# A transformer block on one core: dilated attention without a row maximum, transposes by DMA, and instruction orders fixed beforehand

**The chip, the cores and the metric.** The kernel runs on one core of one Trainium2 chip. The metric is the device time in microseconds (us), the median of several executions. Engines are written as the profile writes them: PE is TensorE (PEld its weight loads), DVE VectorE, ACT ScalarE, POOL GpSimd, SP the engine that issues DMAs. SBUF and PSUM are the on-chip memories in which the code keeps its tiles; here matmuls read from SBUF tiles and write to PSUM tiles. "Span" is the time from the first to the last record of one profiled execution. PEclk is the share of full clock speed that the throttle granted PE.

## The reference

One block: adaptive layer norm, dilated local attention, output projection with a gated residual, a second adaptive norm, a SiLU MLP and a second gated residual. S = 2048 positions, D = 448, 16 heads of 28, MLP width 1792, everything in bf16.

```python
# cut to what matters; x is A_x, mod the six vectors of silu(c) @ w_mod
h = layernorm(x) * (1 + ca) + sa
q, k, v = split(h @ wqkv)                        # 16 heads of 28
idx = pos[:, None] - 2 * arange(8)[None, :]      # 8 keys: i, i-2, ..., i-14
logits = where(idx >= 0, einsum(q, k[idx]) * 28**-0.5, -1e9)
o = einsum(softmax(logits), v[idx]) @ wo
x = x + ga * o
h = layernorm(x) * (1 + cb) + sb
out = x + gb * (silu(h @ w1) @ w2)
```

An even position looks only at even positions and an odd one only at odd positions. Both kernels use that: each works on two sequences of 1024.

## The kernel before

It splits the even and the odd sequence into blocks of 24 queries that look at 32 keys. A copy spreads four heads over a block-diagonal stationary operand, so a score or value matmul has only 32 columns. The mask is added by a matmul with the identity, the softmax subtracts its row maximum, and DVE transposes values and probabilities.

```python
# attention of one group of four heads, T blocks of 24 queries
nc.tensor.matmul(L[:, 0:T, :], lhsT=ident[:], rhs=mask_bf[...], start=True, stop=False)
for j in range(T):
    nc.tensor.matmul(L[:, j, :], lhsT=S4[:, g, j, :], rhs=kg[:, g, BQ*j:BQ*j+BW], ...)
nc.vector.tensor_reduce(out=mx[:, 0:T], in_=L[:, 0:T, :], axis=AX.X, op=ALU.max)
nc.vector.tensor_tensor(out=xm[...], in0=L[...], in1=mx[...].to_broadcast(...), op=ALU.subtract)
nc.scalar.activation(out=pe[...], in_=xm[...], func=ACTF.Exp, scale=SCALE)
# ... later
nc.vector.tensor_reduce(out=rs[:, 0:T], in_=pe[...], axis=AX.X, op=ALU.add)
nc.vector.reciprocal(out=rs[:, 0:T], in_=rs[:, 0:T])
nc.vector.tensor_tensor(out=pn[...], in0=pe[...], in1=rs[...].to_broadcast(...), op=ALU.mult)
nc.vector.transpose(out=pT[:, 0:T, :], in_=pn[:, 0:T, :])
for j in range(T):
    nc.tensor.matmul(O[:, j, :], lhsT=V4[:, g, j, :], rhs=pT[:, j, :], start=True, stop=True)
# ... cut
```

The set-up scales the weights instead of the activations, before anything uses them, and the first projection comes after all of it:

```python
def late_setup_compute():          # norms of the odd sequence, biases, gates
    ...
    for kt in range(NKT):          # 448 x 1792 weights scaled on ACT
        la(nc.scalar.activation(out=w1_sb[:, kt, :], in_=w1_sb[:, kt, :],
                                func=ACTF.Identity, scale=onep[:, 1, kt:kt+1]))
    ...                            # w2 and wo times their gates on DVE
late_setup_compute()
...
qkv_next = project(0)
for k in range(NGRP + 1):
    ...   # attention of group k, then the MLP of group k-1 as a filler
```

Residuals are added by a matmul with the identity, and the MLP's up projection runs its contraction of 448 as four matmuls of 128 rows, the last of them 64 rows of data and 64 of zeros. Apart from a few chains of dependencies, a scheduler decides the order of each engine.

## Time and profile before

| | before |
|---|---|
| device time, median of four runs | 263.18 us (261.44 to 264.94) |
| span and PEclk of the profiled run | 263.8 us, 0.955 |
| PE / DVE / ACT / POOL busy | 208.8 / 157.2 / 167.4 / 28.7 us |
| first QKV matmul starts | 51.5 us |
| first exponential starts | 65.0 us |
| first MLP matmul starts | 93.2 us |
| last matmul ends | 259.5 us |

The lines themselves stand in the prediction below, taken from the page's 40 slices, from a table of stretches (windows), from the chain of waits and from the groups of instructions. The busy shares alone say little: no engine is over 80%. The landmarks in the lower half cut the span into three: 93.2 us up to the first MLP matmul, 166.3 us from there to the last matmul, and a tail of 4.3 us.

### The profile page before, as it was taken

How to read it: one execution, taken by the hardware profiler on the slowest of the kernel's cores; microseconds unless marked ns; L12 is line 12 of the kernel's file. 1: busy time of each engine (PE TensorE's matmuls, PEld its weight loads, DVE VectorE, ACT ScalarE, POOL GpSimd, SP SyncE). 2: the span in 40 equal slices, each digit the busy share in tenths (PEclk: the TensorE clock that was granted, in tenths of full speed). 3: DMA queues.
4: the chain of work that ended last, by engine and by line, in shares of the span. 5: the costliest groups of instructions: out<-in, count | busy, mean ns of one | idle time of the engine just before them, and what ended most of it. 6: DMA issues, size and time to landing. Idle time of an engine off the chain costs nothing.

```text
span 263.8 us, 4748 instructions
## 1 busy us (share of the span) xinstructions
PE 208.8 (79%) x1902; PEld 131.3 (50%) x1902; DVE 157.2 (60%) x361; ACT 167.4 (63%) x296; POOL 28.7 (11%) x53
## 2 busy tenths in 40 slices
PE   0337425989799289988999969999899565999993
PEld 0336223556466167655655646556675343455651
DVE  5383585579998999589704899028996843000000
ACT  2480376698847856499933999429993548553820
POOL 3860111000000100110001100011001101001001
PEclk9999999999979869999999999999999959599999
DMA  6999400000000100004001030010200030201001
GB/s 227 353 322 312 164 0 0 4 0 2 0 0 2 38 6 2 35 0 62 0 14 42 2 60 2 0 51 6 40 2 17 20 60 15 49 0 46 7 20 35
DMA packets 15840, 13.30 MB, mean 50 GB/s; under 512 B 9225, under 2 KB 13962, under 8 KB 15818
## 3 DMA queue, kind: packets, MB, share of 16 engines
q1 hardware_dynamic: 15050, 11.16, 15.3%
q0 software_dynamic: 768, 1.84, 2.0%
q8 instruction: 15, 0.25, 0.4%
q14 instruction: 7, 0.06, 0.1%
HBM read 9.06 MB, written 1.84 MB: 41 GB/s over the span
## 4 chain that ended last, share of the span: by engine, by line
PE 36%; DVE 27%; issue 19%; ACT 9%; POOL 4%; DMA 3%; POOLq 0%; SPq 0%; ACTq 0%; DVEq 0%
PE ps_h L445 12%; PE ps_y L454 10%; DVE mx L391 4%; PE ps_p L368 3%; DVE xm L393 3%; DVE statsb L180 3%; PE O L422 2%; DVE rs L413 2%; ACT qkv L370 2%; DVE pn L416 2%; PE pst L208 2%; ACT w_sb L333 2%; ACT xn L202 2%; DVE S L380 2%; DMA h2T<-xn 2%
## 5 line engine op out<-in xcount | busy, mean ns | idle before, releaser
L445 PE MATMUL ps_h<-h2T,w_sb 128*128 128x384 bf16 (+1 forms) x336 | 56.1, 325 | 11.4 <-DMA h2T<-xn 6.4
L368 PE MATMUL ps_p<-h1T,w_pad 128*128 128x344 bf16 (+1 forms) x288 | 48.9, 318 | 1.4 <-ACT qkv L370 1.3
L447 ACT ACTIVATE hid<-ps_h,b 128x384 bf16<-128x384 f32 (+1 forms) x84 | 44.0, 547 | 8.9 <-PE ps_h L445 5.9
L445 PEld LDWEIGHTS <-w_sb 128*128 128x128 bf16 x336 | 33.4, 102 | 30.7 <-issue 16.3
L454 PE MATMUL ps_y<-w_sb,hid 128*128 128x448 bf16 x224 | 45.0, 353 | 0.0
L370 ACT ACTIVATE qkv<-ps_p,bq 128x344 bf16<-128x344 f32 (+1 forms) x72 | 35.6, 562 | 4.6 <-PE ps_p L368 4.1
L368 PEld LDWEIGHTS <-w_pad 128*128 128x128 bf16 x288 | 28.3, 100 | 18.2 <-issue 4.2
L454 PEld LDWEIGHTS <-hid 128*128 128x128 bf16 x224 | 21.9, 98 | 19.9
L391 DVE TENSOR_REDUCE mx<-L 128x14 f32<-128x448 f32 (+1 forms) x24 | 14.1, 622 | 28.0 <-PE L L389 27.9
L458 ACT CAST ot<-ps_y 128x448 bf16<-128x448 f32 x16 | 8.5, 532 | 35.0 <-PE ps_y L456 35.0
L202 ACT ACTIVATE xn<-x_all,nmra,rstda 128x448 bf16<-128x448 bf16 x16 | 10.9, 748 | 19.1 <-DVE nmra L190 14.6
L459 POOL DMA_DIRECT2D out_dram<-ot x16 | 9.1, 566 | 124.2 <-ACT ot L458 124.2
L422 PE MATMUL O<-pT,V 128*128 128x32 bf16 x344 | 12.6, 180 | 8.4 <-DVE pT L419 8.4
L434 PE MATMUL ps_o<-wo_pad,oT 128*128 128x448 bf16 x64 | 17.6, 387 | 0.6 <-ACT oT L424 0.6
L422 PEld LDWEIGHTS <-V 128*128 128x128 bf16 x344 | 12.1, 99 | 12.0 <-issue 10.2
L208 PE MATMUL pst<-ident,xn 128*128 128x128 bf16 x64 | 9.3, 308 | 9.7 <-ACT xn L202 8.4
L380 DVE COPY S<-qkv 32x1792 bf16<-32x1792 bf16 (+1 forms) x24 | 14.9, 622 | 1.6 <-ACT qkv L370 1.3
L407 DVE COPY V<-vs 32x1792 bf16<-32x1792 bf16 (+1 forms) x24 | 15.1, 628 | 0.6
L413 DVE TENSOR_REDUCE rs<-pe 128x14 f32<-128x448 f32 (+1 forms) x24 | 14.0, 602 | 1.2 <-ACT pe L396 1.1
L419 DVE STREAM_TRANSPOSE pT<-pn 128x448 bf16<-128x448 bf16 (+1 forms) x24 | 14.6, 634 | 0.1
L416 DVE TENSOR_TENSOR pn<-pe,rs 128x448 bf16<-128x448 f32 (+1 forms) x24 | 14.3, 624 | 0.1
L405 DVE STREAM_TRANSPOSE vs<-qkv 128x448 bf16<-128x448 bf16 (+1 forms) x24 | 14.2, 631 | 0.2
(88 smaller groups left out, 247.0 us busy)
## 6 DMA issues: line engine op xcount, KB each, us to landing
x_all<-in_A_x_dram SPq DMA_DIRECT2D x4, 448.0 KB, 9.5
out_dram<-ot POOLq DMA_DIRECT2D x16, 112.0 KB, 2.0
w_sb<-in_B_w_dram SPq DMA_DIRECT2D x1, 1568.0 KB
wmod_sb<-in_w_mod_dram SPq DMA_DIRECT2D x1, 1344.0 KB
w_sb<-in_B_w_dram SPq DMA_DIRECT2D x1, 1344.0 KB, 11.8
wqkv_st<-in_A_wqkv_dram SPq DMA_DIRECT2D x1, 1008.0 KB
wmod_sb<-in_w_mod_dram SPq DMA_DIRECT2D x1, 672.0 KB, 6.0
wo_pad<-in_A_wo_dram SPq DMA_DIRECT2D x4, 98.0 KB
```

What stands on the lines that cost most here:

```text
L202: wa(nc.scalar.activation(out=xn[:, 0:D], in_=x_all[:, U, :], func=ACTF.Identity, scale=rstd[:, j:j + 1], bias=nmr[:, j:j + 1]))
L368: nc.tensor.matmul(ps[:, 0:wd], lhsT=w_pad[:, kt, typ, g, :], rhs=h1T[:, kt, e0:e0 + wd], start=(kt == 0), stop=(kt == NKT - 1))
L370: nc.scalar.activation(out=tiles[typ][:, g, 0:wd], in_=ps[:, 0:wd], func=ACTF.Identity, bias=bq[:, typ * 4 + g:typ * 4 + g + 1])
L380: nc.vector.tensor_copy(out=_ap4(S4[:, 0, 0, :], 32 * hq, 32 * hq, ((TMAX * 128, NG), (128, T), (1, BW))), in_=_ap4(qg[:, 0, :], 32 * hq, ...
L391: nc.vector.tensor_reduce(out=mx[:, 0:T], in_=L[:, 0:T, :], axis=AX.X, op=ALU.max)
L413: nc.vector.tensor_reduce(out=rs[:, 0:T], in_=pe[:, 0:T, :], axis=AX.X, op=ALU.add)
L416: nc.vector.tensor_tensor(out=pn[:, 0:T, :], in0=pe[:, 0:T, :], in1=rs[:, 0:T].unsqueeze(2).to_broadcast([128, T, BW]), op=ALU.mult)
L422: nc.tensor.matmul(O[:, j, :], lhsT=V4[:, g, j, :], rhs=pT[:, j, :], start=True, stop=True)
L434: nc.tensor.matmul(ps[:, 0:D], lhsT=oT[:, g, n0:n0 + 128], rhs=wo_pad[:, g, :], start=(g == 0), stop=False)
L445: nc.tensor.matmul(ps[:, 0:n], lhsT=w1_sb[:, kt, f * 128:(f + 1) * 128], rhs=h2T[:, kt, c0:c0 + n], start=(kt == 0), stop=(kt == NKT - 1))
L447: ins = nc.scalar.activation(out=hid[:, f, 0:n], in_=ps[:, 0:n], func=ACTF.Silu, bias=b1[:, f:f + 1])
L454: nc.tensor.matmul(ps[:, 0:D], lhsT=hid[:, f, j * 128:(j + 1) * 128], rhs=w2_sb[:, f, :], start=(f == 0), stop=False)
```

## The change

Its intent is to take instructions off PE and DVE, and to leave no engine waiting by chance. The new file shares hardly a line with the old one; these are the pieces that matter, marked as added against what they replace.

```diff
-x_view = A_x...rearrange("(a p two) d -> two a p d", two=2, p=128)
+x_view = A_x...rearrange("(c i p t) d -> c p i (t d)", c=NC, i=2, t=2)  # both parities in one piece
 # scores: one matmul for one head and 112 queries, four heads on four row strips of PE
-    nc.tensor.matmul(L[:, j, :], lhsT=S4[:, g, j, :], rhs=kg[:, g, BQ*j:BQ*j+BW], ...)
-    nc.vector.tensor_reduce(out=mx[...], in_=L[...], axis=AX.X, op=ALU.max)
-    nc.vector.tensor_tensor(out=xm[...], in0=L[...], in1=mx[...], op=ALU.subtract)
-    nc.scalar.activation(out=pe[...], in_=xm[...], func=ACTF.Exp, scale=SCALE)
+    r = 32 * (2 * t + j)
+    T.matmul(held[t][:, j, g*nq:(g+1)*nq], lhsT=qk[r:r+DH, 1, g, par, keys], rhs=qk[r:r+DH, 0, g, par, queries])
+    S.activation(out=out_, in_=ps[...], func=ACTF.Exp, scale=SCALE)         # no row maximum
+    V.tensor_tensor(out=p, in0=p, in1=maskb[...], op=ALU.mult)              # mask of ones and zeros
 # values: a column of ones beside V gives the softmax sum
-    nc.vector.tensor_reduce(out=rs[...], in_=pe[...], axis=AX.X, op=ALU.add)
-    nc.vector.transpose(out=pT[...], in_=pn[...])
+    T.matmul(ps[:, h, 0:DH+1], lhsT=p[:, at:at+128], rhs=v[:, h, 0:DH+1], start=True, stop=True)
+    V.reciprocal(out=r, in_=ps[0:nq, :, DH])
+    V.tensor_tensor(out=box["o"][...], in0=ps[0:nq, :, 0:DH], in1=r..., op=ALU.mult)
+    nc.sync.dma_start_transpose(out=oT[:, :, par, ...], in_=box["o"][0:nq, :])
 # residual: an add on DVE that also gives the sum for the next norm
-    nc.tensor.matmul(ps[:, 0:D], lhsT=ident[:], rhs=x_all[:, U, :], start=False, stop=True)
+    V.scalar_tensor_tensor(out=x_all[:, u+par, :], in0=box["ps"][:, par, 0:D], scalar=1.0,
+                           in1=x_all[:, u+par, :], op0=ALU.mult, op1=ALU.add, accum_out=sums[...])
 # the fourth slice of the contraction (64 rows): two of them, on two halves of PE
+    T.matmul(ps[:, j, :], lhsT=w13[half(j), 128*i:128*i+128], rhs=h[half(j), :, 3, :], ...)
 # ... cut: norms, projections, gates, 11 + 12 throw-away matmuls that warm PE up
+ORDER = "0 4 53 26 27 28 35 1 2 3 40 ..."    # from a search on a model of the engines
+P.emit("" if safe else ORDER)                # "": the order of a list scheduler instead
 # without a maximum a sum could overflow: all sums are checked, and a second program stands behind
+    V.tensor_scalar(out=ok[:], in0=rcf, scalar1=LO, scalar2=None, op0=ALU.is_ge)
 # ... cut
+with tc.If(bad > 0):
+    layer(again, tc, io, True)               # softmax with maximum
```

## The prediction

> **What bounds the kernel now.** I read the 40-slice view first, because a change of this size moves stages and not one wait.
>
> ```profile
> PE   0337425989799289988999969999899565999993
> DVE  5383585579998999589704899028996843000000
> ACT  2480376698847856499933999429993548553820
> PEclk9999999999979869999999999999999959599999
> ```
>
> PE is sparse in the first eight slices, nearly full in the middle and full again in the last six, while DVE is empty at the end: three stages. I cut the windows view at their borders, 57.4 us (first DVE piece of attention) and 221.5 us.
>
> ```profile
> core 0: us, PE busy (x) PEld busy (x) DVE busy (x) ACT busy (x) POOL busy (x), PEclk, DMA share, GB/s
> 0.00:57.40 57.40, 27.54 (x273) 19.80 (x274) 33.00 (x102) 30.92 (x39) 14.48 (x31) 1.00 0.50 159
> 57.40:221.50 164.10, 145.72 (x1448) 92.71 (x1446) 124.04 (x259) 116.03 (x222) 10.88 (x16) 0.95 0.08 19
> 221.50:263.80 42.30, 35.51 (x185) 18.75 (x183) 0.16 (x1) 20.48 (x36) 3.31 (x7) 0.92 0.10 27
> ```
>
> So 57 us are set-up, in which PE is busy half the time and mostly waiting on small work; 164 us are attention and MLP together; 42 us are a last MLP on PE alone. The chain of waits says what holds each.
>
> ```profile
> 11.18 0.71 PE ps_c L238 x13
> ...
> 33.08 3.57 ACT V L306 x4
> ...
> 50.38 5.13 ACT w_sb L333 x3
> ...
> 133.39 2.65 PE ps_y L454 x14
> 136.23 2.65 PE ps_y L454 x14
> ...
> 142.31 1.23 DVE mx L391 x2
> 143.56 0.72 DVE xm L393 x2
> ...
> 151.23 1.14 DVE pn L416 x2
> 152.37 0.60 DVE pT L419
> ```
>
> (start, us, engine, tile, line, count.) In the head the chain runs through scaling weights and zeroing buffers on ACT; the first QKV matmul stands at 51.5 us. In the middle it alternates: MLP matmuls on PE, then some 10 us of softmax on DVE with PE on filler. 14 matmuls of 448 columns start in 2.65 us, 189 ns each; the same group's mean is 353 ns, so about 164 ns of a matmul is tail that the next one covers. I use these spacings below, not the group means.
>
> ```profile
> 108.03 0.86 PE L389 MATMUL L<-qkv,S 128*128 128x32 bf16 x28
> 159.12 8.13 PE ps_h L445 x50
> ```
>
> The first gives (0.86 - 0.18) / 27 = 25 ns for a weight load with a 32-column matmul; the second 163 ns for 384 columns. From 163 to 189 is 0.417 ns a column, so 512 columns are 216 ns, 128 are 56 ns.
>
> **What the Trainium skill says.** "TensorE: Matmul & The Clock Gate", Back-to-back issue gap, has N/2.4 + 2.5 ns: 189 ns at 448, which the trace agrees with. "TensorEngine Tiling (Array Packing)", Key Properties, says that row tiles run independently and that changing the tiling mode drains TensorE; the kernel before has no such tiles, so no run shows it yet, and I rest on it. "ScalarE: Activation LUTs", What ACT_TABLE_LOAD costs, gives 186 ns + 0.833 ns an element, 93 ns more for each pointer operand, and an overlap of 93 ns. The xn activation (448 elements, two pointers) would be 745 ns and takes 748; a plain 448 cast takes 532, a little less than its 559. "VectorE: DVE Perf Modes", Side-by-side, allows tensor_tensor two 16-bit elements a cycle: w2 times its gate, 6272 elements, takes 3.43 us, 0.55 ns each, which agrees.
>
> **The change part by part.** PE first. Before, at these spacings: QKV 192 x 146 + 96 x 156 ns = 43.0; MLP up 48.7; MLP down 42.4; output projection and its residuals 96 x 189 = 18.2; mask matmuls 4.6; score and value matmuls 688 x 25 = 17.2; the rest (transposes, gates, one-column matmuls) about 15. Sum 189 us of a 264 us span; some 75 us are waits and cold clock.
>
> After, from the compiled instruction list. The fourth slice of a 448-long contraction (64 rows) is now run as two matmuls on two halves of the array at once, so 8 cost 7. QK 96 full + 16 pairs = 112 x 216 = 24.2 (keys of one parity only, no 32-for-24 windows). V 63 x 189 = 11.9. Output projection 56 x 189 = 10.6, residual gone into a DVE add. MLP up 196 x 216 = 42.3. MLP down 224 x 189 = 42.4. Scores: 288 matmuls of 28 rows, four at a time, 72 x 50 = 3.6. Values 288 x 25 = 7.2, and the extra column of ones gives the softmax sum. Transposes 64 x 56 = 3.6; gates 1.5; modulation columns 64 x 50 = 3.2. Sum 150.5, 38 less. I count about 101 changes of array mode; at half the 164 ns tail each, an estimate, 8 more: 158.
>
> DVE before was 157 us, of it 8 operations of 0.60 to 0.63 us for each of 24 groups (mx, xm, rs, pn, pT and the copies and transposes for S, V): 115. After, each of 18 blocks has a mask multiply (1792 x 0.55 + fixed = 1.09 by the wo gate row), a reciprocal 0.22 and a normalising multiply 0.62: 18 x 1.93 + 0.3 = 35. Statistics (only of the first norm) 16 x 0.77 = 12, h1 modulation 18 x 0.43 = 8, x1 and output adds 32 x 0.62 = 20, and xn, h2, gates and evacuations about 28. Sum 103. ACT: 32 exponentials of 896 (0.84) and 4 of 1024 (0.95) 30.7, 28 Silus of 1024 26.5, 13 QK evacuations 12.3, 5 V 4.2, 15 xn 9.9, 16 squares 9, seven table loads 9, other 8: 110, from 167. Neither is the bound overall.
>
> By stage. The list fixes each engine's order, so I summed it up to the first MLP matmul. PE has 44.5 us there, of which 3 (32 modulation matmuls, 16 transposes) lie before the first QK matmul; ACT 45; DVE 55. The first QK matmul needs x (first half lands near 3.5 us, as the 448 KB load did at 4.2), 0.84 MB of w_mod and 1.2 MB of wqkv: 2.5 MB. The page's first two slices moved 227 and 353 GB/s, so these are in at 9.5 us, plus about 2 for landing and padding: 12 us against 51.5. This is the largest single gain, some 40 us. From there PE needs 41.5 + 38 mode changes x 0.08 = 44.5, to 57; DVE, starting at 3.5, reaches 58 if it never waits. Three engines so near one another will not all be full, and DVE must wait on GpSimd (its pow takes 0.9 us) and w_mod in the head: I put the first MLP matmul at 64. Then PE has 106 + 63 x 0.08 = 111 us, in which ACT (65) and DVE (48) have room and the MLP's matmuls can fill attention's waits. 64 + 111 = 175; 3 of waits and cold clock; 3 for the last add, store and landing. **181 us**.
>
> Off the path: 26 DMA transposes replace 16. The old ones landed 2.4 us after issue; they replace PE or DVE transposes and lie behind filler. In the last blocks the path score, exponent, mask, values, transpose, projection, norm, transpose, MLP takes some 17 us, and the third MLP chunk (21 us of PE) lies beside it. The sum check and its flag are at the end of the queues and overlap the last 9.9 us of matmuls; the second, safe program is jumped over.
>
> **The rivals.** (1) DVE or ACT takes the bound in the first stage: DVE has 55 us there against PE's 44.5, and the exponents wait for projections. For it: the sums. Against: the order was searched with these durations. Each us that DVE waits moves the end, so 190 to 196. (2) A fixed order is brittle: with five queues in a set order, one late DMA transpose (2.4 us) stops everything behind it, and gaps on PE like those before 217 us bring the low clock that followed them before, where 384-column matmuls start every 0.32 us. That gives 195 to 205. (3) Mode changes cost the whole 164 ns tail: 101 x 0.164 = 17 instead of 8, so 190. If they are hidden, 173. (4) The schedule is as good as the PE sum: 12 + 155 + 3 = 170. (5) The check fails and the safe program runs: well over 300 us; the logits here are of order one and the bounds 1e30 apart, so I give it under 1%.
>
> **Range and chances.** The floor is (4), 170; the likeliest losses are (1) and (3), each about 9, seldom both in full. Eight in ten: 172 to 196. Even (2) stays 20% below 263, so faster is nearly sure.
>
> **What would show it.** First QK matmul near 12 us and first MLP matmul near 64; PE dense from there on with 448-column spacing at 189 ns; the paired 64-row matmuls costing one; DVE near 103 and ACT near 110 us busy; the last DVE add within 3 us of the end. The prediction is wrong if the pairs don't overlap (16 x 0.216 + 9 x 0.189 + 8 x 0.189 + 28 x 0.216 = 13 us more), if the first MLP matmul comes after 75, or if PE after that is under 85% busy.

## The result, and the profile after

The changed kernel took 191.13 us, the median of four runs (190.95 to 191.44), against 263.18 us in the same rounds. The ratio is 0.725, with a 95% interval of 0.721 to 0.729. Ratios here and below are the mean time of one kernel's fast runs over that of the other's of the same rounds, so they are not quite the ratio of the quoted medians. All four runs were fast ones, with PEclk from 0.992 to 0.998.

These are the 40 slices of the changed kernel, one digit for each 4.7 us, in tenths of busy time (PEclk in tenths of full speed).

```profile
PE   7759998889879999999997999979999999999980
DVE  7579989999976630079874401697664022101220
ACT  3145799956976496895736667996189652264000
PEclk9999999999999999999999999999999999999996
```

PE is dense from the fourth slice to the end, and its clock stays at 0.9 or more before the last slice. What was a sparse set-up of eight longer slices is gone: DVE is nearly full through slices 4 to 11, and after that only in two single slices. The same in a table of stretches, cut at the first projection matmul, the first MLP matmul and the last add (busy us of each engine, instructions in brackets, then PEclk, share of the DMA engines and GB/s):

```profile
core 0: us, PE busy (x) PEld busy (x) DVE busy (x) ACT busy (x) POOL busy (x), PEclk, DMA share, GB/s
0.00:13.60 13.60, 9.31 (x72) 4.47 (x74) 8.97 (x31) 4.21 (x7) 5.18 (x26) 1.00 0.86 271
13.60:30.00 16.40, 15.42 (x116) 6.57 (x116) 15.12 (x38) 13.11 (x16) 8.19 (x26) 1.00 1.04 330
30.00:50.00 20.00, 18.22 (x286) 10.38 (x284) 18.92 (x38) 16.34 (x22) 1.40 (x4) 1.00 0.19 45
50.00:65.80 15.80, 14.44 (x128) 6.35 (x124) 11.20 (x23) 10.61 (x19) 2.83 (x7) 1.00 0.29 64
65.80:100.00 34.20, 33.47 (x281) 14.69 (x282) 16.83 (x31) 24.13 (x31) 3.40 (x8) 1.00 0.15 32
100.00:140.00 40.00, 37.78 (x357) 17.55 (x358) 21.66 (x48) 27.16 (x38) 2.84 (x9) 1.00 0.20 49
140.00:184.00 44.00, 43.52 (x223) 18.87 (x221) 9.20 (x21) 18.86 (x23) 2.42 (x7) 1.00 0.12 35
```

From 30 to 50 us DVE is 95% busy (18.92 of 20) and PE 91%: DVE leads there. After 65.8 us PE is 98, 94 and 99% busy in the three rows, 97% together, and DVE and ACT have room. The first row is bound by the loads, with the DMA engines at 0.86. The chain of waits shows what holds each point (start, us, engine, tile, line, count):

```profile
5.22 6.66 DMA wqkv<-in_A_wqkv_dram
...
11.90 0.56 DVE wp L522 x2
...
12.70 0.98 DVE h L492 x2
...
52.85 2.31 DMA oT<-o
...
61.82 2.73 DMA h<-xn
...
107.89 0.54 PE ps_h L759 x4
108.43 2.70 PE ps_h L757 x12
111.13 0.54 PE ps_h L759 x4
...
173.69 9.85 PE ps_y L781 x52
...
183.56 0.62 DVE ot L786
```

The head waits for the attention weights, which land at 11.9 us, and then for two things one after another: their padding (`wp`) and the modulation of the activations (`h`). The chain shows DVE's part of both; ACT shares them, and the first projection matmul itself was released by ACT's part of `h`. The first stage ends in two DMA transposes, of the attention's output (2.31 us) and of the normalised activations (2.73 us). After that the chain is almost all matmuls, to one last add.

| | before | after | change |
|---|---|---|---|
| first projection matmul | 51.5 | 13.6 | -37.9 |
| up to the first MLP matmul | 93.2 | 65.8 | -27.4 |
| first MLP matmul to the end of the last matmul | 166.3 | 117.7 | -48.6 |
| end of the last matmul to the end of the span | 4.3 | 5.6 | +1.3 |
| span of the profiled run | 263.8 | 189.1 | -74.7 |
| PE / DVE / ACT busy | 208.8 / 157.2 / 167.4 | 172.2 / 102.1 / 114.4 | |

The device time of the profiled run after is 190.95 us where its span is 189.1, so 1.85 us lie outside the span.

### The profile page after: what moved, and what is told of

Read it like the earlier page. It is cut to its first block, busy times and chain, and to the rows that moved or that the text cites. A ratio compares the mean times of both kernels' runs of the same rounds, so it can differ in the third digit from the quotient of the medians.

```text
span 189.1 us, 3604 instructions
## 1 busy us (share of the span) xinstructions
PE 172.2 (91%) x1449; PEld 78.9 (42%) x1450; DVE 102.1 (54%) x225; ACT 114.4 (61%) x149; POOL 26.3 (14%) x86
## 4 chain that ended last, share of the span: by engine, by line
PE 53%; DVE 21%; DMA 10%; ACT 4%; POOL 4%; issue 3%; SPq 2%; DVEq 0%
PE ps_h L757 20%; PE ps_y L781 17%; DMA h<-xn 4%; PE ps_h L759 4%; DMA wqkv<-in_A_wqkv_dram 4%; PE ps_qk L587 3%; DVE h L492 3%; DVE p L671 3%; PE ps_wo L731 2%; PE ps_v L611 2%; ACT screp L433 2%; DVE h L514 2%; SPq L307 2%; DVE st L423 2%; POOL rs L440 2%
## 5 line engine op out<-in xcount | busy, mean ns | idle before, releaser
L781 PE MATMUL ps_y<-w,both 128*128 128x448 bf16 x224 | 46.1, 353 | 0.0
L763 ACT ACTIVATE both<-ps_h 128x1024 bf16<-128x1024 f32 x28 | 28.4, 1022 | 23.6 <-PE ps_h L759 15.7
L757 PE MATMUL ps_h<-h,w 128*128 128x512 bf16 x168 | 40.6, 380 | 1.3 <-DVE x_all L734 0.9
L647 ACT ACTIVATE p<-ps_l 128x896 bf16<-128x896 f32 (+1 forms) x36 | 31.3, 936 | 3.3 <-PE ps_l L639 3.1
L781 PEld LDWEIGHTS <-both 128*128 128x128 bf16 x224 | 20.6, 98 | 19.9 <-issue 1.5
L587 PE MATMUL ps_qk<-h,wp 128*128 128x512 bf16 (+1 forms) x128 | 27.3, 380 | 1.6 <-ACT h L490 1.1
L671 DVE TENSOR_TENSOR p<-p,maskb 128x1792 bf16<-128x1792 bf16 (+1 forms) x18 | 19.7, 1101 | 14.9 <-ACT p L647 14.9
L757 PEld LDWEIGHTS <-w 128*128 128x128 bf16 x168 | 15.2, 98 | 23.4 <-issue 7.3
L591 ACT CAST qk<-ps_qk 128x1024 bf16<-128x1024 f32 x13 | 12.9, 1005 | 4.9 <-PE ps_qk L587 4.8
L731 PE MATMUL ps_wo<-wo,oT 128*128 128x448 bf16 (+1 forms) x64 | 13.3, 354 | 1.9 <-DMA oT<-o 1.7
L611 PE MATMUL ps_v<-wqkv,h 128*128 128x448 bf16 (+1 forms) x72 | 14.0, 354 | 0.8 <-ACT v L600 0.5
L514 DVE TENSOR_SCALAR h<-h,modc 64x512 bf16<-64x512 bf16 (+1 forms) x15 | 5.6, 403 | 11.0 <-DMA h<-xn 10.9
L702 DVE RECIPROCAL rc<-ps_o 112x16 f32<-112x16 f32 (+1 forms) x18 | 4.6, 254 | 11.9 <-PE ps_o L697 11.9
## 6 DMA issues: line engine op xcount, KB each, us to landing
w<-in_B_w_dram SPq DMA_DIRECT2D x1, 1344.0 KB, 13.6
```

The costliest lines, as they stand in the source:

```text
L587: T.matmul(ps[:, j, :], lhsT=w.rearrange("p h d -> p (h d)"), rhs=h[rows_of(kk, j), kk, :, 128:128 + CP], start=start, stop=stop)
L591: return [(either(act_ns(1024), dve_ns(1024)), lambda o, ps: copy_on(o)(out=qk[:, :, g, :, s0:s0 + CP], in_=ps[:].rearrange("p j (t s) -> ...
L611: T.matmul(ps[:, par, 0:D], lhsT=h[rows_of(kk, par), kk, par, b0:b0 + 128], rhs=w, start=(kk == ks[0]), stop=(kk == ks[-1]))
L647: S.activation(out=out_, in_=ps[:, :, 0:4 * nq].rearrange("p j (g q) -> p j g q", q=nq), func=ACTF.Exp, scale=SCALE)
L671: V.tensor_tensor(out=p, in0=p, in1=maskb[:, 1 if b == 0 else 0, 0:nq].unsqueeze(1).to_broadcast([128, H, nq]), op=ALU.mult)
L731: T.matmul(ps[:, par, 0:D], lhsT=oT[rows, kk, par, s0:s0 + 128], rhs=wo[rows, par, kk, :], start=(q == qs[0]), stop=(q == qs[-1]))
```

## The experiments

Twelve kernels ran, on three chips; the kernel before, run beside them, had medians of 264.66, 264.31 and 263.79 us there. The changed kernel itself was not repeated in those rounds, so its 191.1 us come from other rounds; the ratios to the kernel before bridge them where there is one. All outputs were correct.

### What the old kernel gains by one part alone

**Softmax without its maximum**, in the kernel before. The mask has to be -200 instead of -1e9, as the padded rows would otherwise sum to zero.

```diff
-MASKVAL = -1.0e9
+MASKVAL = -200.0
-        nc.vector.tensor_reduce(out=mx[:, 0:T], in_=L[:, 0:T, :], axis=AX.X, op=ALU.max)
-        nc.vector.tensor_tensor(out=xm[:, 0:T, :], in0=L[:, 0:T, :], in1=mx[...], op=ALU.subtract)
-        ins = nc.scalar.activation(out=pe[:, 0:T, :], in_=xm[:, 0:T, :], func=ACTF.Exp, scale=SCALE)
+        ins = nc.scalar.activation(out=pe[:, 0:T, :], in_=L[:, 0:T, :], func=ACTF.Exp, scale=SCALE)
```

> The kernel before with one part of the change alone: no row maximum (the exponent reads the logits from PSUM; the mask is -200 so that no sum is zero). That takes 48 of 361 VectorE instructions, 28 us of VectorE, of which mx and xm were 7.5% of the chain, 20 us. Theory (VectorE's softmax is on the path in the middle stage): 245 to 255 us of 263. Rival (TensorE fills those waits or another VectorE step takes their place): 258 to 263.

Measured: 249.84 us (249.15 to 250.38, four runs), ratio 0.946 (0.941 to 0.951), so 14.5 us less. DVE's busy time fell by 26.1 us, from 157.2 to 131.1; a little over half of that reached the end.

**The first projection ahead of the late set-up**, in the kernel before.

```diff
+    qkv_next = project(0)
     late_setup_compute()
-    ... (pools moved up)
-    qkv_next = project(0)
```

> The kernel before with one move: the QKV projection of the first group is issued before the second half of the set-up (norms of the other parity, modulation, scaling of w1, wo, w2), not after it. Its first QKV matmul should come at 30 to 36 us instead of 51.5, the exponents still after the scaling of w1 on ScalarE. Theory (the head is order, not data): 250 to 256 us. Rival (the set-up work is the bound of the head, whatever comes first): 260 to 263.

Measured: 264.04 us (261.34 to 264.99), ratio 0.999 (0.991 to 1.008). The first projection matmul did come at 33.4 us instead of 51.5, and nothing came of it. In the stretch from 57.4 to 93.0 us the table reads, for the kernel before and then for this one (columns as above):

```profile
57.40:93.00 35.60, 28.24 (x315) 18.17 (x312) 34.09 (x67) 26.38 (x50) 0.69 (x1) 0.92 0.04 9
```

```profile
57.40:93.00 35.60, 23.01 (x263) 14.65 (x262) 34.77 (x69) 21.58 (x43) 0.70 (x1) 0.86 0.04 8
```

DVE is full in both (34.1 and 34.8 of 35.6 us). The norms, gates and copies of the set-up are still to be done by DVE, only later, and the first MLP matmul moved from 93.2 to 91.9 us. So the date of the first projection was no loss by itself. That DVE's sum of work held the stage fits: in the version without a maximum that sum is smaller, and the first MLP matmul came at 86.0 us. It is not shown to be all of it, since this kernel's chain of waits runs on PE from 70.5 to 82.5 us.

### What the changed kernel loses when one part is undone

**The searched order**: the same operations, ordered by the list scheduler that is in the file.

```diff
-    P.emit("" if safe else ORDER)
+    P.emit("")
```

> The changed kernel with the same operations in the order that its own greedy list scheduler gives in place of the searched order. Theory (the searched order only takes out waits; TensorE's work, about 165 us with the mode changes, is the same): 197 to 205 us, PE waits more by the difference. Rival 1 (the order is most of the gain): over 220. Rival 2 (order matters little with five queues and buffers): within 2 us of 191.

Measured: 212.84 us (209.67 to 214.31). Two of the four runs were slow ones; the two fast ones have a mean of 210.54 us, 19.4 more than the changed kernel's 191.16. That is more than I had expected. The gaps on PE of over 0.25 us, from 13 us on, sum to 16.8 us instead of 5.9, and the clock fell with them; the table of stretches of this kernel:

```profile
30.00:50.00 20.00, 16.02 (x149) 6.41 (x147) 12.51 (x26) 14.61 (x18) 1.40 (x4) 0.83 0.13 34
```

The trace has 149 matmuls in this stretch where that of the searched order has 286, at a PEclk of 0.83, and DVE, which leads there in the searched order, was busy for 12.5 us instead of 18.9. This order lost twice: by the gaps, 10.9 us more, and by slower matmuls, some 6.9 us (an estimate from the table: 0.17 of this stretch and 0.08 of the 44 us from 140 on). Together that is 17.8 of the 19.4 us.

**Transposes on PE instead of by DMA**, with the list order, as the searched one has no place for them. Compare with the run before.

```diff
-            nc.sync.dma_start_transpose(out=oT[:, :, par, ...], in_=box["o"][0:nq, :])
+            for k in range(KT):
+                T.transpose(box["t"][:, k, 0:nq], box["o"][0:nq, 128*k:128*k+128], ident[0:nq, 0:nq])
+            copy_on(o)(out=oT[:, :, par, ...], in_=box["t"][:, :, 0:nq])     # PSUM to SBUF, DVE or ACT
-        nrm.on_dma(h, [mod2])
+        nrm.on_pe(...)                                                       # the second norm likewise
```

> e1_listorder with the 26 DMA transposes (18 of the attention output, 8 of the second norm) made on TensorE instead, with evacuations by ScalarE or VectorE. 136 transposes of 56 ns are 7.6 us of TensorE and 18 evacuations about 9 us of VectorE or ScalarE. Theory (engines' work is the bound, DMA latency is hidden): 6 to 12 us more than e1_listorder. Rival (the 2.3 to 2.7 us of a DMA transpose lie on the path and a TensorE one is shorter): same or 2 to 5 us less.

Measured: 226.29 us (223.26 to 228.0); the two fast runs have a mean of 224.16 us, 13.6 more than with the DMA transposes. PE's busy time rose by 7.4 us (182.0 to 189.4) and DVE's by 7.2 (97.6 to 104.8). I had expected 6 to 12. The list scheduler puts the new operations into an order of its own, and gaps on PE of over 0.25 us rose from 16.8 to 19.9 us, so part of the difference may be the order and not the transposes. A DMA transpose that takes over 2 us to land is still worth having where other work covers it.

**Warm-up matmuls left out.**

```diff
-WARM, JUNK = 11, 3
+WARM, JUNK = 0, 0
```

> The changed kernel without the 23 junk matmuls that keep TensorE busy in the head. Theory (they keep the clock up when QK starts): transposes of the first chunk 0.6 instead of 0.4 us for four and 3 us of QK at the low clock, 192.5 to 194 us. Rival (the first QK matmul waits for wqkv, landed at 11.9 us, and the stage after it is held by VectorE): 191.5 at most.

Measured: 196.89 us (196.51 to 198.66), ratio 0.749 (0.742 to 0.755), 6.1 more by the means. The first projection matmul came only 0.3 us later, but the matmuls behind it were slow, as the theory has it (timeline of PE from 13 to 20 us, this kernel and then the changed one):

```profile
13.88 6.37 PE L587 MATMUL ps_qk<-h,wp 128*128 128x512 bf16 x17 [2.01 <-ACT h L490]
```

```profile
14.23 5.98 PE L587 MATMUL ps_qk<-h,wp 128*128 128x512 bf16 x29 [0.29 <-ACT h L490]
```

Up to 19.4 us they start every 0.427 us, then every 0.216. The table of stretches calls the clock 1.00 there all the same: this run's record of the clock begins only at 19.4 us. That cost some 2.7 us, of which 1.7 are left at the first MLP matmul. Most is lost later: 121.7 us instead of 117.7 between the first MLP matmul and the last matmul. The stretch from 100 to 140 us has a PEclk of 0.96, about 1.6 us, and a gap on PE that was 0.86 us before an MLP group has become 2.40; all gaps over 0.25 us in this stage sum to 4.8 us instead of 2.6. The order was made for a certain start, and a shift there met other waits downstream; which shift made which gap is not settled by this run.

**The pairs of 64-row slices one after another**, on the same half of PE. This kernel and the next also leave the sum check out, so they are compared with the run after them.

```diff
-    w13 = ct([128, F // 2], "w13")
+    w13 = ct([128, F], "w13")
-    T.matmul(ps[:, j, :], lhsT=w13[half(j), 128*i:128*i+128], rhs=h[half(j), :, 3, :], ...)
+    T.matmul(ps[:, j, :], lhsT=w13[half(0), 128*(i+7*j):128*(i+7*j)+128], rhs=h[half(0), :, 3, :], ...)
```

> e2_nocheck with the 64-row slices of the MLP's first matmul all on the same half of the array, so that the two of a pair cannot run at once; the list of instructions is the same. Theory (pairs overlap, PE is the bound): 28 x 0.216 = 6 us more than e2_nocheck, 4.5 at least. Rival 1 (the pairs never overlapped): no difference. Rival 2 (PE has slack in the stages with the MLP): 1 to 2 us more.

Measured: 195.69 us (195.52 to 197.09), ratio 0.744 (0.738 to 0.750). From the first MLP matmul to the last matmul it took 124.0 us, 6.5 more than the 117.5 of the kernel without the check. The 28 pairs of the MLP would cost 28 x 0.216 = 6.0 us if they ran side by side before and one after another now. So they do run side by side.

**The fourth slice as a full matmul** of 128 rows with zeros: no halves of PE and no mode changes in the MLP, but 28 matmuls more.

```diff
-    T.matmul(ps[:, j, :], lhsT=w13[half(j), 128*i:128*i+128], rhs=h[half(j), :, 3, :], ...)
+    T.matmul(ps[:, j, :], lhsT=w13[:, 128*(i+7*j):128*(i+7*j)+128], rhs=h[:, :, 3, :], ...)
```

> e2_nocheck with the same slices as full-height matmuls on zero-padded rows: 28 x 0.216 = 6.0 us more array time, but 32 changes of array mode fewer. If a change costs 0.107 us, as I read from the spacing after the change, 2.6 us more than e2_nocheck; at 0.164, the whole tail, 0.8 more; if changes are free, 6 more.

Measured: 193.2 us (193.01 to 196.33, one of the four runs slow), ratio 0.732 (0.725 to 0.739). The stretch between the same landmarks took 120.3 us, 2.8 more than without the check alone. It pays 6.0 us for the matmuls and saves 32 mode changes: (6.0 - 2.8) / 32 = 0.10 us each. The chain shown above gives the same by itself: four half matmuls and twelve full ones have a period of 111.13 - 107.89 = 3.24 us, where fourteen matmuls at 0.216 are 3.02; the difference of 0.22 covers two changes of mode, 0.11 each.

**No check, no branch.**

```diff
-        ck = P.op(("dve", 1550.0), sums_ok, rc_done)
+        ck = P.op(("dve", 1550.0), none, rc_done)
         ...                                       # likewise for the other three steps
-    with tc.If(bad > 0):
-        with ExitStack() as again:
-            layer(again, tc, io, True)
```

> The changed kernel without the check of the sums, without its flag loads and without the branch to the safe program. Theory (the end is longer than predicted because flag loads, branches and the waits before the branch stand behind the last add): 188 to 189.5 us, 2 to 3 less than the 191.1 of the changed kernel, and the gap from the last add to the end of the span falls from 4.9 to about 3 us. Rival (that end is what every program has, the check is hidden): 191 us, within 0.3.

The edit, which the two runs before it contain too, also keeps two small buffers (`c4`, `sc4`) inside that of the gates.

Measured: median 191.49 us (189.26 to 192.67). Two of the runs were slow ones (192.12 and 192.67, at a PEclk of 0.97); the fast ones were 189.26 and 190.85. So one of them lies in the range I had expected and one does not, and the mean of the two, 190.06, is 1.1 us under the changed kernel, with too few runs for an interval. In the profiled run the tail after the last add did fall as expected, from 4.9 to 2.8 us, but the first MLP matmul came 2.3 us later. The chain of waits of this kernel and of the changed one, at the same output projection:

```profile
56.32 2.59 PE ps_wo L729 x7
```

```profile
55.30 1.60 PE ps_wo L731 x7
```

The seven matmuls took 2.59 us instead of 1.60, because the clock was low there: in this kernel PEclk is 0.89 from 50 to 65.8 us. The check costs 2.1 us of tail, which is shown; that leaving it out makes the kernel faster by as much is not.

**The second program alone**, the one with the maximum, as if the check had failed at once. It is a run of one, so its state is unknown.

```diff
-            bad = layer(first, tc, io, False)
-    with tc.If(bad > 0): ...
+            layer(first, tc, io, True)
```

> The safe program alone, without the fast one: the same layer with queries as rows, a row maximum, the mask added, and the weights transposed back on TensorE, in its list order. For each of 36 half blocks VectorE gets an add from PSUM, a maximum, a subtraction and an evacuation of 1024 elements, about 1.1 us each, less a mask multiplication of 1.09 for each of 18: 103 + 158 - 20 = 241 us of VectorE. Theory (VectorE then bounds it, so leaving out the row maximum is the condition for the rest): 255 to 300 us, no better than the kernel before. Rival (TensorE stays the bound): under 230.

Measured: 436.03 us, far over what I had expected. DVE's busy time was 247.7 us, near what I had reckoned, but that is only 57% of the span of 434.3. The shares of the chain by engine say why:

```profile
DVE 42%; PE 34%; ACT 12%; issue 5%; DMA 4%; POOL 1%; SPq 0%; ACTq 0%; DVEq 0%; POOLq 0%
```

The chain hops between three engines. PEclk was 0.70. A likely reason, not tested by a run: this program has one buffer each for the shifted scores and for the exponentials, so add, maximum, subtraction, exponential and transposes of one block stand in line behind those of the block before. A sum of busy times is a floor, and here it was a poor one. The changed kernel doesn't run this program with these inputs; the branch jumps over it.

### Three attempts to beat the changed kernel

**Weights of Q and K loaded ahead of those of V**, since the head waited for them.

```diff
-    ld_v = [...]
     ld_qk = [...]
+    ld_v = [...]
```

> The changed kernel with one edit: the loads of the Q and K weights go ahead of those of the V weights. Theory (the first QK matmul waits for padded Q and K weights, landed at 11.9 us, and what the head gains is kept): landing at about 10.5 us, first QK matmul near 13.0 instead of 13.6, 0.5 to 1.4 us less in the end. Rival (the head then waits for the first chunk's norm and transposes, done at 12.1 us, and the rest of the order stands still): within 0.3 us of 191.1.

Measured: 190.62 us (190.02 to 191.51, five runs), ratio 0.722 (0.720 to 0.725). The first projection matmul came at 12.9 instead of 13.6 us, but the first MLP matmul at 66.2 instead of 65.8 in the profiled run. The weights were padded by 11.7 us, but the head then waited for the transposes of the normalised activations, which end at 12.1 us. Half a microsecond by the medians, and an interval that overlaps the changed kernel's: not a clear gain.

**The gate on the MLP's down weights on GpSimd**, to relieve DVE in the stretch from 30 to 65 us where it leads. The order was edited to let GpSimd start early.

```diff
-            w2_gated = [P.op(("dve", 535.0), lambda o, f=f: V.tensor_tensor(out=w2[:, f:f+2, :], ...
+            w2_gated = [P.op(("pool", 535.0), lambda o, f=f: G.tensor_tensor(out=w2[:, f:f+2, :], ...
```

> The changed kernel with the seven multiplications of w2 by its gate (4.1 us of VectorE, 2.4 of them before the first MLP matmul) on GpSimd, which is idle from 31 to 58 us, all in that gap. Theory (VectorE, 93% busy from 13.6 to 50 us, holds the first stage): first MLP matmul 1.5 to 2.4 us earlier than 65.8 and the end 1.5 to 2.5 us earlier. Rival 1 (TensorE holds that stage too): 0 to 0.7 us. Rival 2 (GpSimd's large multiplications get in VectorE's way): later than before by 1 us or more.

Measured: 194.28 us (193.63 to 195.51, six runs), ratio 0.738 (0.735 to 0.741), 3.2 us slower. The timeline of DVE (start, us, engine, line, operation, tiles), in this kernel while GpSimd's multiplications ran from 37.6 to 52.6 us, and then in the changed kernel:

```profile
37.85 1.96 DVE L453 TENSOR_SCALAR xn<-x_all,mv,rs 128x448 bf16<-128x448 bf16 x1
39.74 1.21 DVE L591 CAST qk<-ps_qk 128x1024 bf16<-128x1024 f32 x1
...
44.26 2.03 DVE L577 COPY h<-h 128x768 bf16<-128x768 bf16 x1
```

```profile
37.15 0.39 DVE L453 TENSOR_SCALAR xn<-x_all,mv,rs 128x448 bf16<-128x448 bf16 x1
37.45 1.22 DVE L591 CAST qk<-ps_qk 128x1024 bf16<-128x1024 f32 x1
...
42.30 0.35 DVE L577 COPY h<-h 128x768 bf16<-128x768 bf16 x1
```

The same instructions took five times as long or more, 1.96 and 2.03 us instead of 0.39 and 0.35, about one GpSimd multiplication (2.17 us by its group's mean). Each ended within 0.3 us of the end of the multiplication that it ran beside (39.69 and 46.07 us). The cast in between, which reads PSUM, took 1.21 us in both. The Trainium skill, "SBUF — State Buffer", Who interferes with whom, says just this: a copy or a tensor-scalar in a mode that uses both ports waits for the whole of GpSimd's instruction, and an instruction with at most one input in SBUF outside these modes does not. The mask multiply, with both inputs in SBUF, is in its list too, and took 1.82 us here instead of 1.08.

**Both edits together.**

> Both edits of i1_swap and i2_pool. Theory (independent): the sum of the two, 2 to 4 us less than 191.1. Rival (the same wait counted twice): no more than the better of the two.

Measured: 193.54 us (193.13 to 194.19, five runs), ratio 0.734 (0.731 to 0.736): slower again, and nearly what the two parts sum to (+3.2 and -0.5 on 191.1 give 193.8).

No version clearly beats the changed kernel.

## Why the prediction was right, and where it was not

The predicted time was 181.0 us, the range 172 to 196; it took 191.1, so the range held it and "faster" was right. The central value was 10 us low. The profiled run is told apart by the prediction's own stages:

| stage | predicted | measured | difference |
|---|---|---|---|
| first projection matmul | 12 | 13.6 | +1.6 |
| from there to the first MLP matmul | 52 | 52.2 | +0.2 |
| from there to the last matmul | 111 + 3 | 117.7 | +3.7 |
| last add, store, landing | 3 | 5.6 | +2.6 |
| device time beyond the span | 0 | 1.85 | +1.85 |
| sum | 181 | 190.95 | +9.95 |

**The head.** "[T]hese are in at 9.5 us" was early: 237 GB/s over the first 9.5 us are 2.25 MB, not 2.5, and the attention weights landed at 11.9. The 1.7 us from there to the first matmul, padding and then modulation, are within the 2 us that I had given to landing and padding.

**The first stage** came out within 0.2 us. DVE was predicted to lead there and to wait a little on GpSimd and the loads, and the table of stretches shows it at 95% from 30 to 50 us. The sums behind it held: up to the first MLP matmul the table gives DVE 54.2 us, where I had 55, and ACT 44.3, where I had 45. I take the exact agreement as luck within the step "I put the first MLP matmul at 64", which was a judgement and not a sum. The transposes that I had put "Off the path" were on the chain to that matmul, with 2.31 and 2.73 us; what they cost is not shown, as PE was 91% busy from 50 to 65.8 us all the same.

**The MLP stage** was mis-sized above all in the mode changes. By the order of the matmuls in the trace there are 66, not 63, and at 0.107 us instead of 0.08 they cost 7.1 us instead of 5.0. Scores and values were sized rightly. At 77.4 us a group of sixteen scores adds 0.40 us between the matmuls around it; two mode changes are in that, so 0.19 are left, where my step had four times 0.05 = 0.20. At 131.9 us sixteen value matmuls with no mode change beside them add 0.40, as 16 x 0.025 says. The idle time of PE in this stage is 3.1 us, near the 3 that I gave it. That leaves about 1.5 of the 3.7 us without a place; some of it is the tail of 0.16 us that each wait uncovers. The mechanism, PE's own sum from the first MLP matmul on, was right: PE is 97% busy there.

**The spacing of matmuls.** The section of the Trainium skill that I took N/2.4 + 2.5 ns from ("TensorE: Matmul & The Clock Gate", Back-to-back issue gap) gives it for an isolated matmul, and about 131 ns for 512 columns in a stream. This trace has the stream at the formula's figure: twelve of 512 columns take 2.70 us in the chain above, 0.216 us from start to start.

**The tail** was under-counted. The last add ends 0.7 us after the last matmul, as predicted, but 4.9 us follow. "The sum check and its flag ... overlap the last 9.9 us of matmuls" is right for the instructions and wrong for the branch: without it the tail is 2.8 us.

**Device time and span** were treated as one. They differ by 1.85 us in the profiled runs of both this kernel and the one without the check (190.85 and 189.0), so a time predicted from a span has to add it.

**The engines' sums** held: 103 us predicted for DVE and 102.1 measured, 110 and 114.4 for ACT. Most of ACT's difference is a row that I had not foreseen in the groups of instructions:

```profile
L433 ACT ACTIVATION_READ_ACCUMULATOR screp<-x_all,mv 128x1 f32 x16 | 3.1, 192 | 0.0
```

**The step that failed** is "This is the largest single gain, some 40 us", on the first projection matmul at 12 us instead of 51.5. That matmul did move by 38 us, but by the first MLP matmul only 27.4 us of it were left, and the stage after that gave 48.6. The prediction's own sum had it: 64 us against 93.2 is a gain of 29, of 82 in all. The experiment on the old kernel makes the point sharper: the same matmul moved 18 us forward there, and the time did not change. There the head was not a delay that this reordering could lift. What the runs together point to is less work on DVE (157.2 to 102.1 us) and on PE (208.8 to 172.2), and an order in which the rest is seldom in the way. The maximum alone was worth 14.5 us in the old kernel, the DMA transposes 13.6 with the list order and the searched order 19.4. These do not add up to the change, since each was measured in another surrounding.

**The rivals.** That DVE bounds the first stage was right in kind, but cost nothing beyond the 64 us that had it built in. The brittle order is real, as the two experiments on the start and on the check show, but in the form handed over it didn't strike: the gaps on PE are 5.9 us in all. Mode changes at their whole tail of 0.164 us fell; so did hidden ones. "The pairs don't overlap" was excluded for the MLP by experiment, and for the projections by the trace: at 89.41 us two 64-row matmuls of a projection start 0.003 us apart, and the next two 0.22 us later. The changed kernel did not run its safe program, which alone took 436 us, "well over 300" as said.

**Left open.** The split of even and odd positions into one load and the sums inside the adds were not undone by themselves, so their share is not known. Nor is it settled why the kernel without its check had a cold stretch before its first MLP matmul; a gap of 0.9 us on PE comes before it, but the changed kernel has one as long there and no cold stretch.

## What to carry to other kernels

Before a late start is called a loss, look at which engine is full in the stretch after it: in the old kernel DVE was, bringing the start forward only moved its work, and taking work away helped. The searched order is worth a tenth of this kernel's time, but it is tuned to its durations: here earlier weights, a missing check and a missing warm-up each came to the first MLP matmul later than the changed kernel did (by 0.4, 2.3 and 1.7 us), so search again after an edit. When a time is built up from a profile, add what lies outside the sums: mode changes, a branch at the end, and the distance from span to device time.

## What the Trainium skill lacked or had wrong

- "TensorEngine Tiling (Array Packing)", Key Properties, says that a change of tiling mode drains PE but gives no size. The runs show 0.10 to 0.11 us each, from the period of the MLP's groups (3.24 us against 3.02) and from the kernel without halves (+2.8 us where 28 matmuls of 0.216 were added and 32 changes removed).
- "TensorE: Matmul & The Clock Gate", Part 4: PE-mode transpose, gives about 275 ns for a 128x128 transpose in a kernel and says that the fast clock doesn't engage for it. In the changed kernel sixteen in a row take 1.05 us and one record is 0.22 us long, so they follow each other every (1.05 - 0.22) / 15 = 0.055 us, which is what the spacings of 384 and 448 columns give for an ordinary matmul of 128 columns (0.056 us, in the prediction). In the kernel without warm-up eight of them at 10.8 us follow each other every 0.107 us, so they too are faster at the faster clock.
- "SBUF — State Buffer", Who interferes with whom, agrees with the runs, and these add a size: a copy of 0.35 us took 2.03 beside GpSimd multiplications of about 2.2 us.
- No page that I looked up has the cost of reading an accumulated sum: 192 ns for each on ACT (16 of them, 3.1 us) and 83 ns on DVE.
- No page that I looked up has the distance between span and device time, 1.85 us in these runs.
